# Attention, gated mixing and two dense layers on one core: all pairs of heads run before the dense layers instead of among them

## The chip, the cores and the metric

The kernel runs on one core of a Trainium2 chip. Its time is the device time of one execution in microseconds (us). The version before takes 784.71 us, the median of three runs (782.33 to 784.92). The engines are named as the profile names them: PE (TensorE, matmuls), PEld (its weight loads), DVE (VectorE), ACT (ScalarE), POOL (GpSimd) and SP (the queue that issues most transfers).

## What is computed

Four batches of 448 tokens, 12 heads of 64 channels. Sigmoid attention gives x; a causal convolution of 5 taps makes a gate on x; the gated projection goes through `w_out`; a token mixer and a channel MLP follow, each with a residual.

```python
scores = q @ k.T / sqrt(64) - log(448)           # per batch and head
x = sigmoid(scores) @ v                          # (4, 448, 768) after joining the heads
gate = sigmoid(conv5(x, conv_w))                 # depthwise, causal
x2 = (gate * (x @ w_val)) @ w_out
h  = relu(x2.T @ w_tok1) @ w_tok2                # 448 -> 256 -> 448, over tokens
u  = x2 + h.T
out = u + relu(u @ w_ch1) @ w_ch2                # 768 -> 1536 -> 768, over channels
```

The six weight matrices come as 64-bit words in memory and are decoded on the chip.

## The kernel before

Two heads make a pair; a batch has 6 pairs, all four have 24 (`NPT`). For a pair, `scores` (L235) does, for each of three chunks of 128 keys, two fp32 matmuls that use 64 of PE's 128 rows each, and a sigmoid on ACT (L232); `scores_last` (L244) does the remaining 64 keys of two pairs. `av` (L254) and `av_last` (L264) multiply by v into a PSUM tile `psy`, and `evict` (L272) moves the result to an `xb` tile. An fp32 matmul shows as two records in the trace.

A dense product is done in fp32r with each operand split into a high and a low part: three matmuls for one. `proj` (L354) is the projection by `w_val` (`sel` 0, "val") or `w_out` (`sel` 1); one column block j takes 18 matmuls, issued in three parts. `transp` (L395), `tok1` (L409) and `tok2` (L422) are the token mixer. `dense_steps(b)` (L350) lists these steps for a batch: the six val blocks, then w_out blocks, transposes, tok1 and tok2; the last three tok2 steps are carried into the next batch.

A weight of 128 rows is decoded by `decode_parts` (L103) in four parts: masks (three DVE instructions), rebase (one ACT), low (three DVE), high (one ACT). 18 tiles belong to `w_val`, `w_out`, `w_tok1` and `w_tok2`; the 24 tiles of the channel MLP are decoded later by `dec_ch` (L711). The x of a pair goes through `post_parts` (L315): convolution (`conv`, five DVE instructions), a split (ACT high, DVE low) and the gate's sigmoid.

The order of work is written by hand in a table `PLAN` (L25), by pairs: pairs 0 to 11 in `lead` (L552), two pairs a turn, with decoding between and the convolution of batch 0; pairs 12 to 15 in `lead_val` (L610) with the val blocks of batch 0 and the rest of the decoding; pairs 16 to 18 with the rest of batch 0; 19 to 21 with batch 1; 22 and 23 with batch 2; then val of batch 3. `weave` (L495) deals dense steps out between the pairs, `post` (L502) does the convolutions of later batches. From pair 6 on, x goes to memory (`xscr`, L284, on SP) and comes back (`x_back`, L309).

PSUM in `lead` has three double tiles for scores and two `psy` tiles. From pair 12 on, there are two double tiles for scores (`psa`), two `psy` tiles, and two tiles (`psd`) for dense steps. The steps of batch 3 behind val run in the tail, with six tiles (`psw`, L762); there the decoding of the first three blocks of channel weights (`CHAN_LEFT`) and the first channel products are placed among them. The channel MLP (`ch1` L728, `ch2` L744) follows for 4 batches of 12 blocks.

`lead` and `lead_val` stand under `tc.manual_schedule()`: each engine gets its instructions in the order written. Behind it the scheduler orders them by priority.

```python
    with tc.high_priority(-CHAN_LOW):
        for fc in range(CHAN_LEFT):
            dec_ch(fc, early if fc == 0 else ())
    for n, (_, fn) in enumerate(os):
        if n in CHAN_AT:
            ch1(0, 0, *CHAN_AT[n])
        fn()
```

Of the kernel before, what the change touches and what calls it, by code (L numbers as in the profile page):

```python
# [18 lines left out]
A_BUFS = 3  # L19
Q_BUFS = 3  # L20
# [18 lines left out]
def tile_kernel(ctx, tc, qT, kT, v, w_val, conv_w, w_out, w_tok1, w_tok2, w_ch1, w_ch2, out):  # L39
# [163 lines left out]
    def load_qk(i):  # L203
        b, p = divmod(i, NP)
        h0 = 2 * p
        q = attn.tile([P, S], F32, tag="q", bufs=Q_BUFS, name="q")
        k = attn.tile([P, S], F32, tag="k", bufs=Q_BUFS, name="k")
# [19 lines left out]
    def sigmoid(ps, tag, bufs):  # L227
        if tag == "g":
            a = f(mid.tile([P, 2, S], F32R, tag="g", bufs=6, name="ga"))
        else:  # L230
            a = attn.tile([P, 2, S], F32, tag=tag, bufs=bufs, name=tag)
# [3 lines left out]
    def scores(i, c, lead=False):  # L235
        q, k = qk_t[i]
        ps = pa["pool"].tile([P, 2, 512], F32, tag="s", bufs=pa["s"], name="pss")
# [3 lines left out]
        a_t[i, c] = sigmoid(ps, "g", 6) if lead else sigmoid(ps, "a", A_BUFS)  # L241


    def scores_last(i):  # L244
        ps = pa["pool"].tile([P, 2, 512], F32, tag="s", bufs=pa["s"], name="psl")
# [6 lines left out]
        a_t[i, NF] = sigmoid(ps, "al", 1)  # L252

    def av(i):  # L254
        vn = v_t.pop(i)
        y = pa["pool"].tile([P, 512], F32, tag="y", bufs=2, name="psy")
# [15 lines left out]
    def evict(i, on_vector=False, stays=False):  # L272
        y = y_t.pop(i)[:, :S]
        t = attn.tile([P, PAD + S], F32, tag="xb", bufs=4, name="xb")
# [8 lines left out]
        if not stays:  # L283
            nc.sync.dma_start(xscr[i], x)  # L284
            posts.append(i)

    def step_av(i):
        av(i)
        if i % 2:
            av_last(i - 1)  # L290
            evict(i - 1)
            evict(i)

    def step_loads(i):
        if i + 2 < NPT:
            load_v(i + 2)
        if i % 2 and i + 1 < NPT:
            load_vl(i + 1)

    def step_scores(i):  # L300
        n = i + 1
        if n == NPT:
            return [], []
        todo = [lambda c=c: scores(n, c) for c in range(NF)]
        if i % 2:
            todo = [lambda: scores_last(n)] + todo
        return todo[:2], todo[2:]

    def x_back(i):  # L309
        x = attn.tile([P, PAD + S], F32, tag="xb", bufs=4, name="xb")  # L310
        nc.gpsimd.memset(x[:, :PAD], 0.0)
        nc.sync.dma_start(x[:, PAD:], xscr[i])
        x_t[i] = x

    def post_parts(i):  # L315
# [6 lines left out]
        def conv():  # L322
            nc.vector.tensor_scalar(
                out=acc, in0=x[:, :S], scalar1=cw[:, p * KW : p * KW + 1], scalar2=None, op0=ALU.mult
            )
            for t in range(1, KW):
                nc.vector.scalar_tensor_tensor(  # L327
                    out=acc, in0=x[:, t : t + S], scalar=cw[:, p * KW + t : p * KW + t + 1], in1=acc,
                    op0=ALU.mult, op1=ALU.add,
# [11 lines left out]
        return conv, high, low, last  # L341

    def post_pair(i):
        for part in post_parts(i):
            part()


    carry = []

    def dense_steps(b):  # L350
# [3 lines left out]
        def proj(sel, j, part):  # L354
# [16 lines left out]
            if sel == 0:  # L371
                g = gate_t.pop(b * NP + j)

                gv[j] = t = mid.tile([P, 2, S], F32R, tag="g", bufs=6, name="gv")

                def mul():
                    nc.vector.tensor_tensor(out=g, in0=ps[:, :S], in1=g, op=ALU.mult)  # L377

                def high():
                    nc.scalar.activation(out=t[:, 0], in_=g, func=AF.Copy)  # L380

                def low():
                    nc.vector.tensor_tensor(out=t[:, 1], in0=g, in1=f(t[:, 0]), op=ALU.subtract)

                if dn.get("hold") is None:
                    for fn in (mul, high, low):
                        fn()
                else:
                    dn["hold"].append((mul, high, low))
# [48 lines left out]
        def pj(sel, j):  # L438
            return [(5 if b + sel == 0 else 11, lambda part=part: proj(sel, j, part)) for part in range(3)]

        def tr(j):
            return [(10, lambda: transp(j))]

        def t1(half, t):
            return [(20, lambda: tok1(half, t))]
# [4 lines left out]
        held = [carry.pop(0) for _ in range(len(carry))]  # L450
        steps = []
        for j in range(KD):
            steps += pj(0, j)
            if j in (0, 1, KD - 1) and held:
                steps.append(held.pop(0))
        nval = len(steps)
        steps += pj(1, 0) + pj(1, 1) + tr(0) + pj(1, 2) + tr(1) + pj(1, 3) + tr(2) + pj(1, 4)
        steps += t1(0, 0) + t1(0, 1) + pj(1, 5) + tr(3) + t2(0) + tr(4) + t2(1) + tr(5) + t2(2)
        steps += t1(1, 0) + t1(1, 1)
        if b + 1 < B:  # L460
            carry.extend(t2(3) + t2(4) + t2(5))
        else:
            steps += t2(3) + t2(4) + t2(5)
        return steps, nval
# [4 lines left out]
    decs += [dec_tok1(dec, c) for c in range(NF + 1)] + [dec_tok2(dec, c) for c in range(KT)]  # L469
# [7 lines left out]
    def dec_go():  # L477
        if raws:
            raw, go = raws.pop(0)
            for part in go(raw):  # L480
                part()
            dec_load()

# [6 lines left out]
    pend, posts = [], []  # L490
    total = emitted = 0
    val_done = -1
    back = NP

    def weave(frac):  # L495
        nonlocal emitted
        while pend and (emitted < total * frac or not pend[0][0]):
            n, fn = pend.pop(0)
            emitted += n
            fn()  # L500

    def post(most):  # L502
        nonlocal back
        while posts and most and posts[0] // NP <= val_done + 1:
            i = posts.pop(0)
            while back <= i + 1 and back in posts + [i]:
                x_back(back)
                back += 1
            post_pair(i)
            most -= 1  # L510

    def late():
        while raws:
            dec_go()
        dec.release()
        dn["late"] = tc.alloc_tile_pool(name="late", bufs=1, side="right")

    def mark(b):
        nonlocal val_done
        val_done = b  # L520

    rest_of = {}
    pairs0 = PLAN[0][2]

# [317 lines left out]
```

## Time and profile before

| | |
|---|---|
| runs | 782.33, 784.71, 784.92 us |
| profiled execution, its own time | 784.53 us |
| span of that execution | 782.8 us |
| PE busy | 760.2 us (97%) |
| PEld busy | 604.0 us (77%) |
| DVE busy | 385.1 us (49%) |
| ACT busy | 264.2 us (34%) |
| mean granted TensorE clock | 0.997 |

The profile counts PE as busy from the start of a matmul to its modelled end, and matmuls overlap: 18 records can be 3.65 us or 5.5 us of continuous busy time. How well PE is used is therefore read from how many records lie in a stretch, not from the busy share. Stretches are named below by their start and end in us from the start of the span. The columns of a stretch are: its length, then busy us and number of instructions for PE, PEld, DVE, ACT and POOL, then the granted clock (1.00 is 2.4 GHz, 0.50 is 1.2 GHz), the share of the DMA engines' time, and GB/s.

### The profile page before, as it was taken

To read this page: it belongs to the slowest core of one execution; us is meant where nothing else is said; L and a number is where in the kernel's file an instruction comes from. 1 tells how busy PE (TensorE), PEld (TensorE's weight loads), DVE (VectorE), ACT (ScalarE), POOL (GpSimd) and SP (SyncE) were. 2 spreads that over 40 slices of the span, in tenths; PEclk is the share of its full clock that TensorE was granted. 3 is DMA by queue.
4 is the path that set the end of the run, shared out by engine and by line. 5 is a ranking of instruction groups with operands and counts; after the bars stand their busy time and mean duration, and the time that the engine had idled before them with its cause. 6 is when DMAs were issued, how large, how long until landed. Compare 5 with 4: busy or idle time off the path is not lost.

```text
span 782.8 us, 9546 instructions
## 1 busy us (share of the span) xinstructions
PE 760.2 (97%) x3776; PEld 604.0 (77%) x3776; DVE 385.1 (49%) x671; ACT 264.2 (34%) x397; POOL 26.9 (3%) x67
## 2 busy tenths in 40 slices
PE   7999999999999999999999999999999999999998
PEld 3333556566876688788988998899999999999997
DVE  4987778632631743485696899960003100220002
ACT  6888657433323421332442344430002100200000
POOL 1001110000000000000001000000000000000000
PEclk9999999999999999999999999999999999999999
DMA  8667745112300210213533445460002400050001
GB/s 292 203 191 241 247 129 153 60 49 75 103 23 23 74 36 25 83 58 129 197 123 111 158 166 162 161 212 1 1 0 75 138 1 0 27 174 1 0 1 71
DMA packets 48957, 77.73 MB, mean 99 GB/s; under 512 B 4352, under 2 KB 44304, under 8 KB 48912
## 3 DMA queue, kind: packets, MB, share of 16 engines
q1 hardware_dynamic: 45552, 62.54, 24.7%
q0 software_dynamic: 3360, 14.58, 5.5%
q8 instruction: 30, 0.49, 0.3%
q14 instruction: 15, 0.12, 0.1%
HBM read 61.96 MB, written 15.14 MB: 98 GB/s over the span
## 4 chain that ended last, share of the span: by engine, by line
PE 64%; DVE 15%; issue 13%; DMA 3%; ACT 3%; POOL 1%; SPq 0%; POOLq 0%; DVEq 0%; ACTq 0%
PE psh L734 18%; PE pso L750 18%; PE psd L365 13%; PE psy L261 5%; PE pss L240 4%; DVE gate L327 4%; DVE dec_a L124 2%; PE pst L431 2%; DVE raw L114 2%; PE pst L418 1%; DMA xb<-xscr 1%; DVE wch L128 1%; DVE dec_e L127 1%; DVE dec_a L112 1%; DVE dec_c L113 1%
## 5 line engine op out<-in xcount | busy, mean ns | idle before, releaser
L734 PE MATMUL psh<-us,wch 128*128 128x448 f32 x864 | 184.8, 366 | 0.9 <-ACT wch L136 0.6
L750 PE MATMUL pso<-r,wch 128*128 128x448 f32 x864 | 184.0, 366 | 0.6 <-ACT r L88 0.6
L734 PEld LDWEIGHTS psh<-us,wch 128*128 128x128 f32 x864 | 162.1, 188 | 16.0 <-ACT wch L136 1.6
L750 PEld LDWEIGHTS pso<-r,wch 128*128 128x128 f32 x864 | 162.1, 188 | 14.9 <-ACT r L88 1.0
L90 DVE SCALAR_TENSOR_TENSOR r<-psh,r 128x448 fp32r<-128x448 f32 x48 | 29.9, 624 | 211.0 <-ACT r L88 210.7
L88 ACT ACTIVATE r<-psh 128x448 fp32r<-128x448 f32 x48 | 26.1, 543 | 225.7 <-PE psh L734 225.4
L365 PE MATMUL psd<-gv,w 128*128 128x448 f32 x432 | 95.7, 375 | 4.0 <-ACT x2T L392 2.6
L365 PEld LDWEIGHTS psd<-gv,w 128*128 128x128 f32 x432 | 81.1, 191 | 19.2 <-ACT x2T L392 3.8
L365 PE MATMUL psd<-xs,w 128*128 128x448 f32 x432 | 92.5, 369 | 0.5 <-DVE gate L377 0.5
L365 PEld LDWEIGHTS psd<-xs,w 128*128 128x128 f32 x432 | 80.0, 188 | 15.6 <-issue 5.9
L240 PE MATMUL pss<-q,k 64*128 64x448 f32 x288 | 68.8, 578 | 4.7 <-DMA k<-kT 4.1
L327 DVE SCALAR_TENSOR_TENSOR gate<-xb,cw,gate 128x448 f32<-128x448 f32 x96 | 64.7, 685 | 1.6
L240 PEld LDWEIGHTS pss<-q,k 64*128 64x128 f32 x288 | 25.6, 190 | 40.4 <-issue 17.2
L119 ACT ACTIVATE dec_a<-dec_a,exp_b 128x768 int32<-128x768 int32 (+3 forms) x43 | 37.6, 877 | 48.8 <-DVE dec_a L112 47.2
L124 DVE SCALAR_TENSOR_TENSOR dec_a<-raw,dec_a 128x768 int32<-128x768 int32 (+2 forms) x42 | 37.3, 889 | 14.2 <-ACT dec_a L119 14.2
L232 ACT ACTIVATE a<-pss,bias_s 128x896 f32<-128x896 f32 x36 | 35.0, 1006 | 24.0 <-PE pss L240 21.3
L114 DVE SCALAR_TENSOR_TENSOR raw<-raw,dec_c 128x768 f32<-128x768 uint32 (+2 forms) x42 | 37.6, 895 | 1.2
L261 PE MATMUL psy<-a,v 128*64 128x448 f32 x144 | 34.0, 550 | 1.7 <-ACT a L232 1.7
L232 ACT ACTIVATE ga<-pss,bias_s 128x896 f32<-128x896 f32 x36 | 33.2, 1019 | 4.1 <-PE pss L240 4.1
L377 DVE TENSOR_TENSOR gate<-psd,gate 128x448 f32<-128x448 f32 x24 | 15.0, 623 | 39.6 <-PE psd L365 39.5
L418 PE MATMUL pst<-x,wt1H 128*128 128x384 f32 x112 | 30.2, 339 | 1.7 <-ACT x2T L392 1.0
L136 ACT ACTIVATE wch<-dec_a 128x768 fp32r<-128x768 f32 x24 | 20.3, 846 | 29.6 <-DVE dec_a L124 22.5
(71 smaller groups left out, 607.4 us busy)
## 6 DMA issues: line engine op xcount, KB each, us to landing
raw<-w_ch SPq DMA_DIRECT2D x24, 768.0 KB, 4.4
q<-qT SPq DMA_DIRECT2D x24, 224.0 KB, 3.6
k<-kT SPq DMA_DIRECT2D x24, 224.0 KB, 3.7
uscr<-x2T POOLq DMA_DIRECT2D x24, 224.0 KB, 2.2
u<-uscr SPq DMA_DIRECT2D x24, 224.0 KB, 3.9
ur<-uscr SPq DMA_DIRECT2D x24, 224.0 KB, 3.2
out<-ur SPq DMA_DIRECT2D x24, 224.0 KB, 2.3
v<-v SPq DMA_DIRECT2D x24, 192.0 KB, 2.7
```

What stands on the lines that cost most here:

```text
L90: nc.vector.scalar_tensor_tensor(out=l_out, in0=src, scalar=0.0, in1=f(h_out), op0=ALU.max, op1=ALU.subtract)
L114: nc.vector.scalar_tensor_tensor(out=lo.bitcast(F32), in0=lo.bitcast(U32), scalar=2.0**-32, in1=c, op0=ALU.mult, op1=ALU.add)
L119: nc.scalar.activation(out=t["a"], in_=t["a"], func=AF.Relu, scale=8.0, bias=exp_b)
L124: nc.vector.scalar_tensor_tensor(out=a, in0=hi, scalar=-0x80000000, in1=a, op0=ALU.bitwise_and, op1=ALU.bitwise_or)
L232: nc.scalar.activation(out=a, in_=ps[:, :, :S], func=AF.Sigmoid, bias=bias_s, scale=QK_SCALE)
L240: nc.tensor.matmul(ps[:, j, :S], k[rows, c * P : (c + 1) * P], q[rows], start=True, stop=True)
L261: nc.tensor.matmul(y[cols, :S], vn[:, c, cols], a[:, j], start=c == 0, stop=False)
L327: nc.vector.scalar_tensor_tensor(out=acc, in0=x[:, t : t + S], scalar=cw[:, p * KW + t : p * KW + t + 1], in1=acc, op0=ALU.mult, op1=ALU.add,)
L365: nc.tensor.matmul(ps[:, :S], w(a, kk), s[:, c, :], start=kk == 0 and n == 0, stop=kk == KD - 1 and n == 2,)
L418: nc.tensor.matmul(ps[:, :HALF], a, x[:, m], start=n == 0, stop=n == len(mm) - 1)
L734: nc.tensor.matmul(ps[:, :S], wch[fc][:, 0, a, kk * P : (kk + 1) * P], us_t[b, kk][:, c, :], start=kk == 0 and n == 0, stop=kk == KD - 1 a ...
L750: nc.tensor.matmul(acc[j][:, :S], wch[fc][:, 1, a, j * P : (j + 1) * P], r[:, c, :], start=fc == 0 and n == 0, stop=fc == KF - 1 and n == 2,)
```

## The change

`PLAN`, `lead_val`, `post`, the `hold` list and the carrying of steps are gone. `lead` runs over all 24 pairs, two a turn, in twelve turns, and holds the whole decoding of the 18 tiles (`DEC_LEAD` says how many masks a turn begins); the small tiles of `w_tok1` and `w_tok2` are put between those of `w_out`, so that a turn that begins two has one large and one small tile. All of it, the dense steps of batches 0 to 2 and val of batch 3 included, is now under the manual order.

After the last pair the three double tiles of the scores are given to six tiles `psw` for dense steps. The dense steps of a batch run alone: val, then w_out with the token mixer. The two tok1 steps and three tok2 steps that end a batch are put between the val blocks of the next. Convolutions of batch b + 1 are cut into single instructions and dealt out by weight among the w_out steps of batch b; x comes back from memory four pairs ahead. The tail keeps its text; the channel products take the two `psy` tiles.

```diff
-PLAN = (
-    (None, "", range(0, 12)),
-    (0, "v", range(12, 16)),
-    (0, "o", range(16, 19)),
-    (1, "vo", range(19, 22)),
-    (2, "vo", range(22, 24)),
-    (3, "v", ()),
-)
-DEC_LEAD = (1, 1, 1, 1, 1, 2, 1)
-DEC_VAL = (1, 1, 1, 1, 1, 1, 2, 2)
+DEC_LEAD = (1, 1, 1, 1, 1, 2, 2, 2, 2, 2, 2, 1, 0)
...
+    xbp = tc.alloc_tile_pool(name="xbp", bufs=1, side="left")
-    psl = tc.alloc_tile_pool(name="psl", bufs=2, space=bass.MemoryType.PSUM)
-    pa = {"pool": psl, "s": 3}
+    psy = tc.alloc_tile_pool(name="psy", bufs=2, space=bass.MemoryType.PSUM)
+    pss = tc.alloc_tile_pool(name="pss", bufs=3, space=bass.MemoryType.PSUM)
...
+        val = [pj(0, j) for j in range(KD)]
+        outs = pj(1, 0) + pj(1, 1) + tr(0) + pj(1, 2) + tr(1) + pj(1, 3) + tr(2) + pj(1, 4)
+        outs += t1(0, 0) + t1(0, 1) + pj(1, 5) + tr(3) + t2(0) + tr(4) + t2(1) + tr(5) + t2(2)
+        return val, outs, t1(1, 0) + t1(1, 1), t2(3) + t2(4) + t2(5)
...
-    decs += [dec_tok1(dec, c) for c in range(NF + 1)] + [dec_tok2(dec, c) for c in range(KT)]
+    for n, t in enumerate([dec_tok1(dec, c) for c in range(NF + 1)] + [dec_tok2(dec, c) for c in range(KT)]):
+        decs.insert(6 + 2 * n, t)
...
-        for n, p in enumerate(pairs0[::2]):
+        for n, p in enumerate(range(0, NPT, 2)):
...
             for i in (p, p + 1):
                 evict(i, i > p, p < NP)
             conved = [post_parts(i) for i in (p, p + 1)] if p < NP else []
...
+    def post_ops(b):
+        ops, gates = [], []
+        for i in range(b * NP, (b + 1) * NP):
+            parts = {}
+            def first(i=i, parts=parts):
+                parts["all"] = post_parts(i)
+                parts["all"][0][0]()
+                parts["all"][1]()
+            ops.append(first)
+            for t in range(1, KW):
+                ops.append(lambda t=t, parts=parts: parts["all"][0][t]())
+                if t == 2:
+                    ops += gates
+                    gates = [lambda parts=parts: parts["all"][3]()]
+            def end(i=i, parts=parts):
+                parts["all"][2]()
+                if i + 4 < NPT:
+                    x_back(i + 4)
+            ops.append(end)
+        return ops + gates
+
+    def weave(steps, ops):
+        total = sum(n for n, _ in steps)
+        count, at, done = len(ops), 0, 0
+        for n, fn in steps:
+            fn()
+            at += n
+            while done < count * at // total:
+                ops[done]()
+                done += 1
...
     with tc.manual_schedule():
         lead()
+        pss.release()
+        psw = tc.alloc_tile_pool(name="psw", bufs=6, space=bass.MemoryType.PSUM)
+        pd.update(pool=psw, n=6)
+        attn.release()
+        dec.release()
+        dn["late"] = tc.alloc_tile_pool(name="late", bufs=1, side="right")
+        for i in range(NP, NP + 4):
+            x_back(i)
+        back1, back2 = [], []
+        for b in range(B):
+            val, outs, t1, t2 = dense_steps(b)
+            weave(val[0] + back1 + sum(val[1:], []) + back2, [])
+            if b + 1 < B:
+                weave(outs, post_ops(b + 1))
+            else:
+                os = outs + t1 + t2
+            back1, back2 = t1, t2
+        xbp.release()
...
-            part["ps"] = psd.tile([P, 512], F32, tag="d", bufs=2, name="psh")
+            part["ps"] = psy.tile([P, 512], F32, tag="y", bufs=2, name="psh")
```

## Rows read from the trace of the kernel before

**Rows 1.** Page, busy time by engine: us, share of the span, instructions.
```profile
PE 760.2 (97%) x3776; PEld 604.0 (77%) x3776; DVE 385.1 (49%) x671; ACT 264.2 (34%) x397; POOL 26.9 (3%) x67
```

**Rows 2.** Busy time by stretch: attention, mixed, last dense steps, channels.
```profile
57.24:79.44 22.20, 20.38 (x118) 7.31 (x116) 14.13 (x20) 18.69 (x24) 2.05 (x3) 1.00 0.78 245
79.44:320.95 241.51, 235.99 (x1152) 166.36 (x1152) 122.67 (x237) 95.70 (x149) 13.92 (x36) 0.99 0.25 79
379.68:427.65 47.97, 45.11 (x231) 40.05 (x230) 38.49 (x68) 18.88 (x31) 3.04 (x6) 1.00 0.44 149
427.65:520.00 92.35, 90.81 (x440) 81.81 (x439) 85.45 (x125) 38.22 (x51) 0.96 (x2) 1.00 0.49 162
```

**Rows 3.** Timeline of PE in the lead: start, length, line, tiles, count, [idle before].
```profile
11.34 4.73 PE L261 MATMUL psy<-ga,v 128*64 128x448 f32 x24
...
45.10 4.73 PE L261 MATMUL psy<-ga,v 128*64 128x448 f32 x24
...
57.24 4.73 PE L261 MATMUL psy<-ga,v 128*64 128x448 f32 x24
...
62.70 0.93 PE L251 MATMUL psl<-q,k 64*64 64x448 f32 x8
...
68.50 4.73 PE L261 MATMUL psy<-ga,v 128*64 128x448 f32 x24
```

**Rows 4.** Timeline of ACT in a turn that finishes two large tiles.
```profile
64.69 5.50 ACT L232 ACTIVATE ga<-pss,bias_s 128x896 f32<-128x896 f32 x6
...
74.52 0.84 ACT L136 ACTIVATE w<-dec_a 128x768 fp32r<-128x768 f32 x1 [1.61 <-DVE dec_a L124]
...
76.58 2.81 ACT L232 ACTIVATE a<-pss,bias_s 128x896 f32<-128x896 f32 x3
```

**Rows 5.** Groups by line and shape: the DVE and ACT steps of a small tile.
```profile
L124 DVE SCALAR_TENSOR_TENSOR dec_a<-raw,dec_a 128x256 int32<-128x256 int32 x4 | 1.7, 422 | 0.5 <-ACT dec_a L119 0.5
L136 ACT ACTIVATE wt1H<-dec_a 128x256 fp32r<-128x256 f32 x4 | 1.6, 409 | 1.3 <-DVE dec_a L124 1.3
```

**Rows 6.** Transfers: queue, count, size, median us from issue to landing; and SP's timeline.
```profile
k<-kT SPq DMA_DIRECT2D x24, 224.0 KB, 3.7
raw<-w_tok POOLq DMA_DIRECT2D x3, 256.0 KB, 3.1
...
67.20 0.56 SPq L208 DMA_DIRECT2D q<-qT  x1
```

**Rows 7.** Timeline of PE: dense steps beside attention, and dense steps by themselves.
```profile
83.55 2.71 PE L365 MATMUL psd<-xs,w 128*128 128x448 f32 x12
86.19 1.02 PE L240 MATMUL pss<-q,k 64*128 64x448 f32 x4
...
160.19 5.51 PE L365 MATMUL psd<-gv,w 128*128 128x448 f32 x18 [1.47 <-ACT x2T L392]
...
363.87 14.75 PE L365 MATMUL psd<-xs,w 128*128 128x448 f32 x72
378.45 0.56 PE L431 MATMUL pst<-wt2H,h 128*128 128x448 f32 x2
...
379.68 7.60 PE L365 MATMUL psd<-gv,w 128*128 128x448 f32 x36
387.12 0.60 PE L401 MATMUL pst<-ident,x2T 128*128 128x128 f32 x4
387.48 0.85 PE L365 MATMUL psd<-gv,w 128*128 128x448 f32 x3
```

**Rows 8.** Chain that ended last, in order of time: a tok1 pair and a tok2 step.
```profile
275.60 3.82 PE pst L418 x22
...
291.50 1.23 PE pst L431 x6
```

**Rows 9.** Timeline of DVE: decoding channel weights around the end of val, batch 3.
```profile
353.94 0.56 DVE L112 TENSOR_SCALAR dec_a<-raw 128x768 int32<-128x768 int32 x1 [1.13 <-DMA raw<-w_ch]
...
379.45 0.95 DVE L128 SCALAR_TENSOR_TENSOR wch<-raw,dec_e 128x768 fp32r<-128x768 f32 x1
```

More of the change, by code (lines that the diff above doesn't have):

```diff
@@ L225, in load_vl, with sigmoid, scores @@
         vl_t[i] = t
[L227 to L231, printed above, removed]
+    def sigmoid(ps, a):
         nc.scalar.activation(out=a, in_=ps[:, :, :S], func=AF.Sigmoid, bias=bias_s, scale=QK_SCALE)
         return a
-    def scores(i, c, lead=False):
+    def scores(i, c):
         q, k = qk_t[i]
-        ps = pa["pool"].tile([P, 2, 512], F32, tag="s", bufs=pa["s"], name="pss")
+        ps = pss.tile([P, 2, 512], F32, tag="s", bufs=3, name="pss")
         for j in range(2):
@@ L240, in scores @@
             nc.tensor.matmul(ps[:, j, :S], k[rows, c * P : (c + 1) * P], q[rows], start=True, stop=True)
-        a_t[i, c] = sigmoid(ps, "g", 6) if lead else sigmoid(ps, "a", A_BUFS)
+        a = mid.tile([P, 2, S], F32R, tag="g", bufs=6, name="ga")
+        a_t[i, c] = sigmoid(ps, f(a))
     def scores_last(i):
-        ps = pa["pool"].tile([P, 2, 512], F32, tag="s", bufs=pa["s"], name="psl")
+        ps = pss.tile([P, 2, 512], F32, tag="s", bufs=3, name="psl")
         for h in range(2):
@@ L284, in evict @@
             nc.sync.dma_start(xscr[i], x)
[L285 to L307, printed above, removed]
     def x_back(i):
-        x = attn.tile([P, PAD + S], F32, tag="xb", bufs=4, name="xb")
+        x = xbp.tile([P, PAD + S], F32, tag="xb", bufs=4, name="xb")
         nc.gpsimd.memset(x[:, :PAD], 0.0)
@@ L339, in last @@
             nc.scalar.activation(out=acc, in_=acc, func=AF.Sigmoid)
[L341 to L348, printed above, removed]
+        return [lambda t=t: conv(t) for t in range(KW)], high, low, last
     def dense_steps(b):
@@ L372, in proj @@
                 g = gate_t.pop(b * NP + j)
[L374 to L389, printed above, removed]
+                nc.vector.tensor_tensor(out=g, in0=ps[:, :S], in1=g, op=ALU.mult)
+                gv[j] = mid.tile([P, 2, S], F32R, tag="g", bufs=6, name="gv")
+                split(gv[j][:, 0], gv[j][:, 1], g)
             else:
@@ L489, in tile_kernel @@
     make_identity(nc, ident)
[L490 to L523, printed above, removed]
-    begun, going = [], []
+    begun = []
     def dec_masks(n):
@@ L559, in lead @@
         for c in range(NF):
-            scores(0, c, True)
+            scores(0, c)
         for part in cgo(craw):
@@ L565, in lead @@
         for c in range(NF):
-            scores(1, c, True)
+            scores(1, c)
         load_qk(4)
@@ L577, in lead @@
                 parts[1]()
-            for parts, _ in done:
+            for parts in done:
                 parts[2]()
@@ L584, in lead @@
                 fn()
-            for parts, _ in done:
+            for parts in done:
                 parts[3]()
@@ new lines, in lead @@
+            if more:
+                scores_last(p + 2)
+                for i in (p + 2, p + 3):
+                    for c in range(NF):
+                        scores(i, c)
+                    if i + 3 < NPT:
+                        load_qk(i + 3)
+            for parts in conved:
+                for fn in parts[0]:
+                    fn()
+        assert not (conved or gates or begun or raws or decs)
+    def post_ops(b):
[18 more added lines that the diff above has]
+        return ops + gates
@@ L693, in tile_kernel @@
-    psa.release()
-    attn.release()
+        pss.release()
[12 more added lines that the diff above has]
+                weave(outs, post_ops(b + 1))
+            else:
+                os = outs + t1 + t2
+            back1, back2 = t1, t2
@@ L808, in tile_kernel @@
     pso.release()
-    psd.release()
+    psy.release()
 def kernel(q, k, v, moe_w_val, moe_conv_w, moe_w_out, moe2_w_tok1, moe2_w_tok2, moe2_w_ch1, moe2_w_ch2):
```

166 lines of the change are left out of this document (21 added, 145 removed).

## The prediction

> **What bounds the kernel now.** I read the busy times first [rows 1]: PE is busy 97% of the span, so nothing but PE's own time can give much. But PEld is at 77%, and a busy PE is not a full one, so the second view is the table by stretch [rows 2], read by records per us. In the channel part, from 427.65 to 520, 440 records lie in 92.35 us, 0.210 us each, and each of them is a full dense matmul. In the mixed stretch, 79.44 to 320.95, where attention and dense steps share PE, 1152 lie in 241.51 us, 0.2097 us each, but many of these are the half-size records of attention, transposes and tok1, which cost less elsewhere. The reader should see that this stretch looks full by busy time (235.99 us) and is not.
>
> The third view is PE's timeline, which gives the price of each piece when it is undisturbed. In the lead, three turns of two pairs start 33.76 us apart in all, 11.25 us each, and a later one takes 68.50 - 57.24 = 11.26 us [rows 3]. Dense: 72 val matmuls run from 363.87 to 378.45, 14.58 us, so a val block of 18 is 3.65 us; 36 matmuls by `w_out` run from 379.68 to 387.12, 7.44 us, so a block is 3.72 us; four transposes take 387.48 - 387.12 = 0.36 us [rows 7]; two tok1 steps are 3.82 us, a tok2 step 1.23 us [rows 8]. Beside attention the same 12 val matmuls take 86.19 - 83.55 = 2.64 us instead of 12 x 0.2025 = 2.43, and one block of `w_out` takes over 5 us behind a wait of 1.47 us for ACT [rows 7]. With these prices I can build the stretch of the new order from pieces that the trace has already run.
>
> **The change part by part.** *Attention and decoding, all in the lead.* The first product with v starts at 11.34; nothing ahead of it changes. There are twelve turns; eleven end in scores for the next pairs, and the last has none. A full turn is 11.26 us [rows 3]. One turn of the six before is longer, 57.24 - 45.10 = 12.14 us, 0.88 more; it follows the three turns with convolutions, which stay, so I keep this once. The last turn is av and av_last, 62.70 - 57.24 = 5.46 us [rows 3]. Sum: 11.34 + 11 x 11.26 + 0.88 + 5.46 = 141.5 us.
>
> Whether 11.26 holds for turns 6 to 10, which finish two decoded tiles each, is the first open cost. In a turn of before that finishes two large tiles ACT is the longer chain: its six sigmoids start at 64.69, those of the next pairs at 76.58, 11.89 us, and ahead of the second tile's last step it waits 1.61 us for DVE [rows 4]. In the new order the second tile is small (256 or 448 wide), and its steps on that chain are 0.422 us on DVE and 0.409 us on ACT [rows 5]. The large one's ACT step is 0.84 [rows 4], twice that, and I take the same ratio for its DVE step, so some 0.43 + 0.43 us come off: 11.0 us, under PE's 11.26. PE stays the bound, by 0.2 to 0.3 us.
>
> Behind this stands a second chain. With three `raw` buffers and two tiles a turn, the second tile's load goes out only when the first tile's low part is done, and DVE waits for it ahead of the copy of `psy`; SP's writes of x wait for this copy, and the loads of q and k stand behind them. In the turn of before that begins at 57.24, q goes out at 67.20 and takes 0.56 us to issue, and the k behind it takes 3.7 us to land [rows 3, 6]: 71.5. The next scores that want it come 11.26 + 5.46 us behind 57.24, at 74.0. So there are 2.5 us of room. That turn began two large masks without waiting; one large mask and a wait for a small load, 3.1 us [rows 6], end by my count about 1 us later. The bounds are 0 and, for six turns that each lose 1.5 us, 9 us; I take 1 us, since the rows leave room. Writing x of pairs 12 to 23 and loading tiles for longer stays far from the DMA limit: the lead's stretch shows a DMA share of 0.78 with large tiles only [rows 2].
>
> PE has no gap between the last av and val of batch 0: the scores' PSUM tiles were read before that av could start, the x of batch 0 was convolved in the first turns, and `w_val` is decoded first. I cost this at nothing; a visible wait for the release of the pools would be under 1 us.
>
> *Batches 0 to 2 alone.* Of one batch: 6 x 3.65 (val) + 6 x 3.72 (w_out) + 6 x 0.36 (transposes) + 2 x 3.82 (tok1) + 6 x 1.23 (tok2) = 61.4 us; three are 184.2. To this come waits at transposes and tok steps, which before had attention work to cover them. The nearest row is the last stretch of dense steps [rows 2], which already runs with six PSUM tiles and no attention: 47.97 us, against 43.2 by the prices (the same without val, plus one channel block of 3.65), so 4.8 us are lost. Bounds: 0 to 4.8 per batch, 0 to 14.4 in all. I take 1.5 per batch, 4.5 in all: in that last stretch ACT and DVE also decode channel weights (DVE busy 38.49 of 47.97) in an order that no one wrote, while in batches 0 to 2 they have one convolution instruction at a time between the dense steps. Those convolutions cost PE nothing as long as DVE keeps up, which in the mixed stretch was busy 122.67 us of 241.51 with decoding besides [rows 2]. The wait that they bring to DVE is for x out of memory, with the copies of the dense steps queued behind it and PE behind these. SP issues that load four pairs ahead, two thirds of a batch's w_out steps, and POOL's memset ahead of it stands only behind writes of tok2 results of earlier steps; I cost this wait at nothing. Without that lead it would be one landing, near the 3.7 us of k [rows 6], per pair.
>
> *Val of batch 3 and the tail.* Val is 6 x 3.65 = 21.9 us. The tail keeps its text, so I take its measured 47.97 us, and from 427.65 to the end of the span, 782.76 - 427.65 = 355.1 us. One thing moves: before, DVE started channel weights at 353.94, during val of batch 3, and only the write of the first tile waited to 379.45 [rows 9]. Now val of batch 3 stands in the manual order, and the decoding comes behind it on DVE. Six tiles at 85.45 us / 18 = 4.7 us [rows 2] are 28 us; some 4 to 5 us of that move into the last dense stretch, which has 47.97 - 38.49 = 9.5 us of DVE idle. I cost it at nothing, with bounds of -2 (loads come earlier) and +5.
>
> Sum: 141.5 + 1 + 184.2 + 4.5 + 21.9 + 47.97 + 355.1 = 756.2 us of span; the profiled run took 1.73 us beyond its span (784.53 and 782.8), which gives 757.9, so 758 us. The profiled run lies within 0.2 us of the median, so no further shift.
>
> The drain of PE fits this: 12 matmuls beside attention lose 0.21 us [rows 7]. The Trainium skill (TensorEngine Tiling (Array Packing), "Key Properties") says that changing the tiling mode drains the engine, and attention's half arrays are such a mode. By the rule the change saves one drain wherever attention and dense steps alternated; the sum above holds these savings already, through the undisturbed prices.
>
> **The rivals.** *Stalls of dense steps alone.* If batches 0 to 2 lose what the last stretch lost, 4.8 us each, 9.9 us are added: 768. For it: transposes follow their projection by one block only, with nothing else to run. Against it: the waits there are behind decoding.
>
> *The lead starves.* If q and k come late in turns 5 to 10, at 1.5 to 2 us each, 9 to 12 us are added: 768 to 770.
>
> *Decoding becomes the bound, no change.* If the scheduler places the six first tiles of channel weights behind all of batch 3's dense steps, PE waits for 28 us of decoding, less the 3.65 us of a channel block: 758 + 25 = 783. For it: the decoding has lower priority and its early start is gone. Against it: DVE's idle time in that stretch and the same text of the tail.
>
> *The clock falls, slower.* Attention alone fills half of the array per matmul. If the granted clock fell to 1.2 GHz in the 62 us of attention that the change adds to the lead (79 to 141 us), every us of work there would cost another: up to 820 us. It decides from 27 us at half clock on, the whole gain. Against it: the lead's rows show 1.00 with attention only, and the mixed stretch, the one with gaps, shows 0.99 [rows 2]. The Trainium skill (TensorE: Matmul & The Clock Gate, "What's actually happening") has it that the throttled clock is the default and activity releases it; the trace agrees, 1.00 where PE runs without gaps.
>
> **How the numbers follow.** Forecast, 750 to 764: 0.60. Stalls, about 768: 0.15. Lead starves, about 769: 0.10. Both or more, 774 to 782: 0.03. Decoding, about 783: 0.05. Clock, 790 and above: 0.07. The likeliest is 758. The range goes from 750 (no waits, and the tail 2 to 3 us better) to 774 (either of the first two rivals with decoding 5 us late); it leaves out the last three and a little below. A measurement of this kernel tells about 0.3% from no change, 2.4 us: faster 0.88, same 0.05, slower 0.07.
>
> **What would show it.** PE's last av near 141 us; turns 11.3 us apart to the end, and ACT's sigmoids starting 0.2 us behind the scores; val of batch 0 right behind; the batches 62 to 63 us apart; the last tok2 near 400 us; the channel part 355 us as before. Wrong would be: turns of 12.5 us with PE waiting for q, k or ACT; dense steps with waits of over a us at each transpose; channel matmuls that wait for DVE behind 400 us; a granted clock of 0.50 before 141 us.

## The result, and the profile after

The changed kernel takes 756.89 us (median of four runs, 754.59 to 758.20) against 784.25 us for the kernel before on the same chip (four runs): a ratio of 0.9652, with a 95% interval from 0.9621 to 0.9682. Its profiled execution took 756.25 us, with a span of 754.5 us; before, the span was 782.8 us. The gain of 28.3 us of span is the difference that the text below accounts for.

The busy times by engine from the page of the changed kernel answer to [rows 1]. PE's busy time fell by 19.2 us although it runs the same 3776 matmuls, DVE's rose by 8.5 us, and the others' changed by less than 4:

```profile
PE 741.0 (98%) x3776; PEld 604.3 (80%) x3776; DVE 393.6 (52%) x677; ACT 260.3 (35%) x391; POOL 27.5 (4%) x67
```

The same table by stretch as [rows 2], for the stretches of the changed kernel: attention from the first product with v, the dense steps of batches 0 to 2 with val of batch 3, the last dense steps, and the first part of the channel products.

```profile
12.87:143.60 130.73, 130.56 (x739) 47.97 (x737) 92.07 (x159) 108.26 (x138) 10.51 (x18) 1.00 0.69 215
143.60:353.74 210.14, 207.79 (x1073) 192.15 (x1069) 136.40 (x254) 63.66 (x120) 10.33 (x31) 1.00 0.18 57
353.74:399.25 45.51, 44.28 (x232) 40.28 (x230) 37.14 (x66) 16.92 (x27) 4.17 (x8) 1.00 0.45 154
399.25:491.00 91.75, 89.71 (x436) 81.25 (x435) 85.12 (x124) 38.45 (x51) 0.96 (x2) 1.00 0.49 161
```

The reader sees two uniform stages where there was one mixed stretch. The last dense step ends at 399.25 instead of 427.65, 28.4 us sooner; from there to the end it is 355.25 us, before 355.1. So the whole gain lies ahead of the end of the dense steps.

PE's timeline shows the hand-over from attention to dense work and the clean prices of the dense steps, as [rows 7] did for before:

```profile
138.03 4.73 PE L248 MATMUL psy<-ga,v 128*64 128x448 f32 x24
142.69 0.98 PE L257 MATMUL psy<-al,vl 64*64 64x448 f32 x8
143.60 2.70 PE L321 MATMUL psd<-xs,w 128*128 128x448 f32 x12
...
165.59 7.59 PE L321 MATMUL psd<-gv,w 128*128 128x448 f32 x36
173.02 0.60 PE L344 MATMUL pst<-ident,x2T 128*128 128x128 f32 x4
173.37 0.45 PE L321 MATMUL psd<-gv,w 128*128 128x448 f32 x1
```

Val of batch 0 starts 0.91 us after the last group of attention did, with no wait. The 108 val matmuls take 21.99 us, and four transposes 0.35 us. One wait comes back in each of batches 1 to 3, in the first val block, which takes 4.70 us instead of 3.65; 0.78 us of the 1.05 show as a wait:

```profile
197.85 3.61 PE L321 MATMUL psd<-xs,w 128*128 128x448 f32 x17
202.24 0.47 PE L321 MATMUL psd<-xs,w 128*128 128x448 f32 x1 [0.78 <-DVE xs L299]
202.55 0.34 PE L361 MATMUL pst<-x,wt1H 128*128 128x384 f32 x1
```

From the records of PE I also counted where before lost its time. Each group of matmuls is priced at the undisturbed rate of its kind, and what it took beyond that is lost. In the mixed stretch (79.44 to 320.95) this is 24.6 us. In it, PE goes 62 times from attention to dense work or back. Groups ending in such a change that lost under 0.6 us each sum to 11.5 us; six single losses of 0.85 to 2.1 us sum to 9.1; the rest is 4.0. From 320.95 to 427.65 another 9.9 us are lost, none of them at a change. After, the dense steps from 143.6 to 399.25 lose 6.2 us in all. These sums hang on the prices, the one for the scores above all.

One loss in the mixed stretch is neither a change nor a wait. Two matmuls that each use half of the array run together when they stand side by side, their records starting within 0.01 us of each other. One alone takes as long as the two: in the trace of before, the four records of two `scores` matmuls and the two records of a single one both take 0.95 us up to the next matmul.

```profile
86.19 1.02 PE L240 MATMUL pss<-q,k 64*128 64x448 f32 x4
87.14 2.70 PE L365 MATMUL psd<-xs,w 128*128 128x448 f32 x12
...
179.78 1.02 PE L240 MATMUL pss<-q,k 64*128 64x448 f32 x2
180.73 0.68 PE L431 MATMUL pst<-wt2H,h 128*128 128x448 f32 x2
```

In the mixed stretch 14 matmuls of attention run alone like this, in the lead of either kernel none. At some 0.38 us each (half of what two cost in the run lump below) that is about 5 of the 24.6 us, an estimate; some 2.5 of them stand within the 11.5 above.

### The profile page after: what moved, and what is told of

The parts are those of the page before. It is cut to its first block, busy times and chain, and to the rows that moved or that the text cites. A ratio compares the mean times of both kernels' runs of the same rounds, so it can differ in the third digit from the quotient of the medians.

```text
span 754.5 us, 9599 instructions
## 1 busy us (share of the span) xinstructions
PE 741.0 (98%) x3776; PEld 604.3 (80%) x3776; DVE 393.6 (52%) x677; ACT 260.3 (35%) x391; POOL 27.5 (4%) x67
## 4 chain that ended last, share of the span: by engine, by line
PE 67%; DVE 14%; issue 13%; DMA 3%; ACT 1%; POOL 1%; SPq 0%; POOLq 0%; DVEq 0%; ACTq 0%
PE psh L582 19%; PE pso L598 18%; PE psd L321 15%; PE pss L226 6%; PE psy L248 5%; DVE gate L291 3%; PE pst L361 2%; DMA raw<-w_ch 2%; DVE raw L102 2%; DVE dec_a L112 2%; DVE wch L116 1%; PE psl L238 1%; DVE dec_a L100 1%; PE pst L374 1%; PE psy L257 1%
## 5 line engine op out<-in xcount | busy, mean ns | idle before, releaser
L321 PE MATMUL psd<-gv,w 128*128 128x448 f32 x432 | 92.8, 369 | 0.0
L321 PE MATMUL psd<-xs,w 128*128 128x448 f32 x432 | 89.6, 366 | 2.3 <-DVE xs L299 2.3
L217 ACT ACTIVATE ga<-pss,bias_s 128x896 f32<-128x896 f32 x72 | 66.4, 1019 | 4.7 <-PE pss L226 4.7
L226 PE MATMUL pss<-q,k 64*128 64x448 f32 x288 | 63.0, 579 | 4.3 <-DMA k<-kT 4.1
L248 PE MATMUL psy<-ga,v 128*64 128x448 f32 x288 | 56.8, 543 | 0.0
L248 PEld LDWEIGHTS psy<-ga,v 128*64 128x64 f32 x288 | 19.6, 137 | 35.7 <-issue 29.9
L76 ACT ACTIVATE gv<-gate 128x448 fp32r<-128x448 f32 x24 | 13.8, 577 | 61.7 <-DVE gate L330 61.7
```

What stands on the lines that cost most here:

```text
L76: nc.scalar.activation(out=h_out, in_=src, func=AF.Relu if relu else AF.Copy)
L226: nc.tensor.matmul(ps[:, j, :S], k[rows, c * P : (c + 1) * P], q[rows], start=True, stop=True)
L248: nc.tensor.matmul(y[cols, :S], vn[:, c, cols], a[:, j], start=c == 0, stop=False)
L321: nc.tensor.matmul(ps[:, :S], w(a, kk), s[:, c, :], start=kk == 0 and n == 0, stop=kk == KD - 1 and n == 2,)
```

## The experiments

All times are medians of four runs. The kernel before, run beside them, had medians from 782.94 to 785.11 us.

| label | what is changed | us | ratio to before (95%) |
|---|---|---|---|
| (the change) | | 756.89 | 0.9652 (0.9621 to 0.9682) |
| lump | 36 added matmuls in one group | 770.96 | 0.9839 (0.9818 to 0.9860) |
| spread | the same, dealt out | 777.32 | 0.9918 (0.9897 to 0.9939) |
| psum2 | two PSUM tiles for dense steps | 769.06 | 0.9818 (0.9797 to 0.9838) |
| psum3 | three | 757.99 | 0.9673 (0.9659 to 0.9688) |
| spread2 | spread and psum2 together | 790.22 | 1.0071 (1.0052 to 1.0090) |
| bigpairs | small tiles decoded last | 759.50 | 0.9690 (0.9667 to 0.9714) |
| whole | convolutions in one piece | 778.15 | 0.9919 (0.9898 to 0.9940) |
| beforehand | before, ordered by hand | 831.32 | 1.0599 (1.0565 to 1.0632) |
| autodense | dense steps ordered by the scheduler | 752.82 | 0.9604 (0.9579 to 0.9628) |
| sooner | convolutions end sooner | 752.84 | 0.9602 (0.9588 to 0.9616) |
| low0 | sooner, channel decoding not lower | 753.33 | 0.9604 (0.9583 to 0.9626) |

The theory was that before lost time on PE itself, at each change between attention and dense work, and through waits that mixed work brings. The rivals were that the gain is the number of PSUM tiles, or the order by hand.

### What a change between attention and dense work costs: lump and spread

```diff
+    def extra(n):
+        m = xs_t[0]
+        for _ in range(n):
+            for j in range(2):
+                rows = slice(j * D, (j + 1) * D)
+                nc.tensor.matmul(spare[j][:, :S], ident[rows], f(m[rows, 0, :]), start=True, stop=True)
...
+            if b == 0:
+                extra(18)                                     # lump
...
+                val = [[(n, lambda fn=fn: (extra(1), fn())) for n, fn in v] for v in val]   # spread
```

> The changed kernel with 36 added fp32 matmuls of 64 rows (72 records) on PE in one group ahead of val of batch 0; their results are not used. No engine waits for them and they wait for none. Both theories: 72 x 0.206 = 14.8 us more, 771 to 773 us.

> The same 36 added matmuls, two ahead of each of the 18 parts of val of batch 0, so that PE changes between half-array and full-array matmuls 36 times. Theory (each alternation costs PE itself some 0.185 us; 62 of them in the mixed stretch of before would be 11.5 of its 24.6 lost us): 6 to 7 us over the kernel with one group, 777 to 780 us. Rival (alternation is free; all that was lost were waits for buffers and other engines): the same as one group within 1 us.

Measured: 770.96 and 777.32 us, 6.4 us apart; the spans of the profiled executions, 769.1 and 775.8, are 6.7 apart. Lump costs 14.1 us, just under what was expected. In both kernels the first added matmul does wait once, 0.72 us, for a copy out of `psy`. PE's timeline in lump:

```profile
143.52 13.85 PE L529 MATMUL spare<-xs,ident 64*128 64x448 f32 x72 [0.72 <-ACT xb L269]
157.30 22.15 PE L321 MATMUL psd<-xs,w 128*128 128x448 f32 x108
179.29 3.04 PE L321 MATMUL psd<-gv,w 128*128 128x448 f32 x14
```

and in spread:

```profile
147.14 1.48 PE L321 MATMUL psd<-xs,w 128*128 128x448 f32 x6
148.55 1.02 PE L529 MATMUL spare<-xs,ident 64*128 64x448 f32 x4
149.51 0.47 PE L321 MATMUL psd<-xs,w 128*128 128x448 f32 x1
```

In one group, a half-array record takes 13.78 / 72 = 0.191 us and a dense one 21.99 / 108 = 0.2036. Alternating, four and six take 149.51 - 147.14 = 2.37 us instead of 4 x 0.191 + 6 x 0.2036 = 1.99. That is 0.38 us for two changes, 0.19 us each, with no wait on any engine shown. The rival is out: alternation is not free. Dealt out, PE changes 35 times instead of once, 34 times more and not 36 as expected, so 6.4 to 6.7 us are 0.19 to 0.20 us a change. 62 changes at that price are 11.6 to 12.2 us, and the mixed stretch of before lost 11.5 at its changes, or some 9, by the same prices, without the matmuls that ran alone. The added matmuls have the form of the scores (64*128); changes to and from the products with v (128*64) were not tried by themselves.

### The PSUM tiles: psum2, psum3, spread2

```diff
-        psw = tc.alloc_tile_pool(name="psw", bufs=6, space=bass.MemoryType.PSUM)
-        pd.update(pool=psw, n=6)
+        psw = tc.alloc_tile_pool(name="psw", bufs=2, space=bass.MemoryType.PSUM)
+        pd.update(pool=psw, n=2)
...
         xbp.release()
+        psw.release()
+        psw = tc.alloc_tile_pool(name="psw", bufs=6, space=bass.MemoryType.PSUM)
+        pd.update(pool=psw, n=6)
```

> The changed kernel with two PSUM tiles instead of six for the dense steps up to val of batch 3; everything else stays. Theory (most of the gain is the order: no alternation of attention and dense steps on PE, and waits that the order hides): some waits come back at the transposes and tok steps of batches 0 to 2, as in the stretch from 320.95 to 379.68 of before, 1 to 3 us a batch, 3 to 9 us in all, 760 to 766 us. Rival (the gain is mostly the third and following PSUM tiles): 15 us or more come back, 772 to 785 us.

Measured: 769.06 us, 12.2 more than with six tiles, between what the two expected. PE's timeline of this kernel shows where:

```profile
173.39 0.60 PE L344 MATMUL pst<-ident,x2T 128*128 128x128 f32 x4
174.19 1.08 PE L321 MATMUL psd<-gv,w 128*128 128x448 f32 x4 [0.20 <-ACT x2T L335]
...
197.41 0.63 PE L344 MATMUL pst<-ident,x2T 128*128 128x128 f32 x4 [0.49 <-DVE x L348]
198.69 0.67 PE L374 MATMUL pst<-wt2H,h 128*128 128x448 f32 x2 [0.65 <-DVE x2T L378]
```

Four transposes keep PE for 0.80 us until the next block, not 0.36, because that block's tile is still being copied by ACT; in the chain of transposes and tok2 steps each waits for the copy of the step before the last. A batch takes 66.2 us instead of 62.7.

> The changed kernel with three PSUM tiles instead of six for the dense steps up to val of batch 3. Two tiles gave 769.1 us, 12.2 more than six, 3.5 us a batch at the transposes (0.80 us for four instead of 0.36) and the tok2 steps. Theory (with two tiles a step waits for the copy of the step before the last; one more tile covers a copy of 0.6 us): nearly all of it goes with the third tile, 757 to 760 us. Rival (each further tile gives its share): 765 to 767 us.

Measured: 757.99 us. The third tile takes back nearly all, 11.1 of 12.2 us; the rival, a share for each tile, is out.

> The kernel with the 36 added matmuls dealt out among val of batch 0 (777.3 us) and, besides, two PSUM tiles instead of six for the dense steps up to val of batch 3 (769.1 us alone, 12.2 over the changed kernel's 756.9). Theory (alternation and tiles are separate costs): they add, 777.3 + 12.2 = 789.5, 788 to 791 us; then 62 alternations at 0.187 us and two tiles, 11.6 + 12.2, account for 24 of the 27 to 28 us between the two kernels. Rival (one hides the other, as PE's extra time at each change covers the wait for a tile): 783 to 786 us.

Measured: 790.22 us, 12.9 over spread. The two costs add. That this is no faster than the kernel before says little, since 14.1 us of it are the added matmuls themselves (lump). Together 11.6 and 12.2 us are 23.8 of the 27.4 us between the kernels. This sum is a reconstruction and not shown: the 12.2 us are the price of two tiles in the new order, and no run has more than two with attention among the dense steps. The count on the traces divides the gain otherwise: 24.6 + 9.9 - 6.2 = 28.3 us, as much as the spans differ by, of which some 9 lie at changes, about 5 in matmuls that ran alone, and the rest in waits and small losses.

### The decoding in the lead: bigpairs

```diff
-    for n, t in enumerate([dec_tok1(dec, c) for c in range(NF + 1)] + [dec_tok2(dec, c) for c in range(KT)]):
-        decs.insert(6 + 2 * n, t)
+    decs += [dec_tok1(dec, c) for c in range(NF + 1)] + [dec_tok2(dec, c) for c in range(KT)]
```

> The changed kernel with the small tiles of w_tok1 and w_tok2 decoded last, as before the change, so that some turns of the lead finish two large tiles. The prediction's step: such a turn is bound by ACT and DVE, 11.9 us instead of 11.26, and the second large tile's load (5 us) comes late for its masks, so three or four turns of 11.9 to 13.5 us, 2 to 7 us more in all, 759 to 764 us. Rival (PE alone sets the turn, whatever is decoded): no change.

Measured: 759.50 us, 2.6 more. The runs go from 757.45 to 761.85 and the interval of the ratio overlaps that of the change, so this is not clear of noise. The profiled execution is the slowest of the four. Its table by stretch, one turn a row:

```profile
58.55:69.81 11.26, 11.26 (x66) 4.18 (x65) 6.82 (x10) 9.57 (x13) 0.77 (x1) 1.00 0.79 252
69.81:81.69 11.88, 11.74 (x66) 4.04 (x64) 7.41 (x11) 10.05 (x13) 1.29 (x2) 1.00 0.74 252
81.69:93.59 11.90, 11.90 (x66) 4.27 (x64) 8.71 (x12) 10.06 (x13) 1.30 (x2) 1.00 0.80 255
93.59:108.76 15.17, 13.13 (x67) 4.68 (x65) 10.68 (x17) 10.36 (x13) 1.32 (x2) 0.89 0.68 214
108.76:120.02 11.26, 11.26 (x66) 4.19 (x64) 5.12 (x12) 9.34 (x13) 1.58 (x3) 1.00 0.65 187
```

Two turns take 11.88 and 11.90 us, as the chain of ACT in [rows 4] gave (11.89); their sigmoids start 89.78 - 77.88 = 11.90 us apart. The third takes 15.17. There the second chain has run out of room. DVE waits 4.23 us for a tile, and the copy of `psy` stands behind its masks. PE's next product with v starts 0.10 us after that copy ends; the profile names no releaser for it (`issue`), so that it waited for the copy is read from the order. The granted clock then falls in the same turn, after PE had waited for 2.04 us. The rows of the timeline, of ACT, DVE and PE:

```profile
77.88 5.50 ACT L217 ACTIVATE ga<-pss,bias_s 128x896 f32<-128x896 f32 x6
89.78 5.50 ACT L217 ACTIVATE ga<-pss,bias_s 128x896 f32<-128x896 f32 x6
...
95.44 0.57 DVE L100 TENSOR_SCALAR dec_a<-raw 128x768 int32<-128x768 int32 x1 [4.23 <-DMA raw<-w_out]
97.39 0.62 DVE L267 COPY xb<-psy 128x448 f32<-128x448 f32 x1
...
98.11 4.05 PE L248 MATMUL psy<-ga,v 128*64 128x448 f32 x12 [2.04 <-issue]
```

So PE is not alone in setting the turn: two turns lose 1.3 us together, as the prediction's step worked out. The third turn's 3.9 us are one execution's; it is the only one of the four with a mean clock under 1.00 (0.998).

### Who orders, and in what pieces: beforehand, autodense, sooner, whole

Beforehand puts the mixed stretch of the kernel before under the manual order:

```diff
-    for b, parts, pairs in PLAN[2:]:
+    with tc.manual_schedule():
+        for b, parts, pairs in PLAN[2:]:
...
```

> The kernel before with the mixed stretch from pair 16 to val of batch 3 under the manual order too, in the order in which its text issues it; nothing else is changed. Theory (alternation and waits of mixed work make the difference, not who orders): 780 to 792 us, the 62 alternations still there. Rival (the scheduler's order of the mixed stretch was what the change removed): 770 us or less.

Measured: 831.32 us, which neither expected; it lies 39 us above the theory's upper end. The text's order of mixed work is far worse than the scheduler's. Part of it is the clock: the mean granted clock of the execution is 0.964, against 0.997, so some 60 of 831 us ran at 1.2 GHz (2 x 0.036 x 831). That would cost 30 us if PE had worked all through them; by the records it sat idle for some 17 of them, which leaves about 20 us, an estimate. PE's idle time grew by more, from 22.6 us of the span (782.8 - 760.2) to 59.1 (831.0 - 771.9). Two stretches of 40 us from the table show it beside PE's lower busy time:

```profile
120.00:160.00 40.00, 33.58 (x150) 23.86 (x152) 31.42 (x62) 17.71 (x31) 1.15 (x5) 0.87 0.24 70
160.00:200.00 40.00, 31.67 (x152) 22.13 (x144) 10.34 (x21) 14.27 (x22) 1.19 (x3) 0.87 0.22 69
```

One cause is in ACT's timeline:

```profile
143.39 0.58 ACT L339 ACTIVATE gate<-gate 128x448 f32<-128x448 f32 x1 [2.74 <-DVE gate L327]
143.88 0.96 ACT L392 ACTIVATE x2T<-psd 128x448 f32<-128x448 f32 x2
```

and it is the largest row of the list of PE's waits (us in total, times, longest):

```profile
PE psd L365 <- ACT x2T L392: 17.4, 5, 7.7
```

ACT waits 2.74 us for a convolution on DVE ahead of the gate's sigmoid; the copies of two dense results stand behind it, and PE waits for those. In the text a pair's convolution and its sigmoid are one piece.

Whole puts the convolutions of the changed kernel back into such pieces, and changes nothing else:

```diff
-                if t == 2:
-                    ops += gates
-                    gates = [lambda parts=parts: parts["all"][3]()]
...
             ops.append(end)
-        return ops + gates
+            ops.append(lambda parts=parts: parts["all"][3]())
+            group = ops[-6 - 1 :]
+            ops[-6 - 1 :] = [lambda group=group: [fn() for fn in group]]
+        return ops
```

> The changed kernel with the convolution of a pair put among the w_out steps in one piece (five DVE instructions, low part, and the gate's sigmoid on ACT right behind) instead of in single instructions with the sigmoid held back; the same work, six pieces a batch. In the kernel before with its mixed stretch ordered by hand (831.3 us), ACT waits up to 2.7 us for such a group and the copies of the dense steps stand behind it. Theory (cutting the convolution is what makes an order by hand cheap here): PE waits 0.5 to 2 us at several steps of each batch, 8 to 25 us in all, 765 to 782 us. Rival (with no attention among them the dense steps have slack enough for whole pieces): 757 to 760 us.

Measured: 778.15 us, 21.3 more: most of the gain is lost. ACT's timeline:

```profile
179.99 0.58 ACT L302 ACTIVATE gate<-gate 128x448 f32<-128x448 f32 x1 [3.10 <-DVE gate L291]
180.47 0.58 ACT L346 ACTIVATE x<-pst 128x512 fp32r<-128x512 f32 x1
180.95 0.54 ACT L335 ACTIVATE x2T<-psd 128x448 f32<-128x448 f32 x1
```

The first two rows of the list of PE's waits:

```profile
PE psd L321 <- DVE xs L299: 10.6, 3, 3.5
PE psd L321 <- ACT x L346: 4.5, 3, 1.5
```

The six tiles cover ACT's 3.10 us there (PE shows no wait near 180), but the last piece of a batch ends far behind the w_out steps, and PE waits up to 3.5 us in the first val block; the mean clock is 0.988. Set beside the changed kernel record by record, PE loses nothing through the first three pieces of a batch. Behind the fourth and the fifth, among the last transposes and tok2 steps, it loses 0.9 and 1.7 us more, at the sixth 2.7, and the clock of 1.2 GHz that follows costs 1.4 to 2.4: 6.8 to 7.8 us a batch. So it is shown that whole pieces at the end of a batch cost 21.3 us, more than the alternation or the tiles alone. Whether whole pieces would cost this too if they ended sooner, as in the kernel sooner below, was not tried, so that the cutting by itself is a condition of the new order is not shown.

Autodense takes the dense steps out of the manual order, by moving their code out of the block:

```diff
     with tc.manual_schedule():
         lead()
-        pss.release()
...
+    pss.release()
...
```

> The changed kernel with only the attention lead in the order written by hand; the dense steps of batches 0 to 2 and val of batch 3 are ordered by the scheduler, as nearly all of them were before. Theory (alternation and waits of the mixed stretch): the order by hand is worth little, 755 to 762 us. Rival (the gain is the order by hand): 770 us or more.

Sooner keeps the order by hand and lets the convolutions end earlier:

```diff
-            while done < count * at // total:
+            while done < min(count, count * at * 10 // (9 * total)):
```

> The changed kernel with the convolution instructions dealt out over the first nine tenths of the w_out steps instead of all of them. In the trace of the changed kernel PE waits 1.05 us in the first val block of batches 1 to 3 (4.70 us instead of 3.65) for the low part of x of the last pair. Theory (that wait is the place of the last convolution instructions in DVE's order): it goes in all three batches, 3 us less, 753 to 754 us. Rival (DVE is behind with work by then, and the place does not matter): no change, 756 to 758 us.

Measured: 752.82 and 752.84 us, both about 4 us faster than the change itself, and the fastest kernels here; autodense came out 2 us below the range of its theory. The first val block of batch 1 in sooner:

```profile
196.65 3.81 PE L321 MATMUL psd<-xs,w 128*128 128x448 f32 x18
200.30 0.34 PE L361 MATMUL pst<-x,wt1H 128*128 128x384 f32 x1
```

It takes 3.65 us, and the same holds in batches 2 and 3: the wait of 1.05 us was the place of the last convolution instructions in DVE's order, and nothing else. These three blocks are 3.1 of the 4 us. In autodense the scheduler moves them, with the same effect. The order of the dense steps by hand is thus not what the change gained by: without it the kernel is faster still.

### What is left in the tail: low0

```diff
-CHAN_LOW = 600
+CHAN_LOW = 0
```

> The changed kernel with the convolution instructions dealt out sooner (752.8 us) and, besides, the decoding of the channel weights at normal priority in the tail instead of 600 lower. PE still loses some 2.5 us in the last dense steps and 4 to 5 us around 460 to 480 of the span, where DVE decodes without a pause. Theory (in that stretch DVE's 18 tiles behind the last dense step set the end; priority does not start them sooner, since their place in memory comes free only then): 752 to 756 us, no gain. Rival (decoding is late because it stands behind other work on DVE): 747 to 750 us.

Measured: 753.33 us, no gain over sooner. In the stretch of the table where PE still loses some 2 us, DVE is busy nearly all the time in both. In sooner:

```profile
455.00:480.00 25.00, 22.84 (x110) 19.99 (x109) 23.14 (x34) 10.85 (x16) 0.00 (x0) 1.00 0.39 128
```

and in low0:

```profile
455.00:480.00 25.00, 22.97 (x107) 19.33 (x106) 22.70 (x34) 11.39 (x16) 0.00 (x0) 1.00 0.39 133
```

This fits decoding as the limit there. That the memory for the tiles comes free too late was not tried.

## Why the prediction was right, step by step

| step | predicted us | measured us |
|---|---|---|
| first product with v | 11.34 | 12.87 |
| eleven turns | 123.86 + 0.88 + 1 | 125.16 |
| last turn | 5.46 | 5.57 |
| batches 0 to 2 and val of batch 3 | 184.2 + 4.5 + 21.9 = 210.6 | 210.14 |
| last dense steps | 47.97 | 45.51 |
| channel products to the end | 355.1 | 355.25 |
| span | 756.2 | 754.5 |

**The method held.** The new order is made of pieces that before had already run undisturbed, and nine of its eleven turns and its blocks take what [rows 3, 7, 8] said, to 0.1 us. The forecast, 758, is 1.1 us off the median. That it came so close is in part luck: the start was 1.5 us longer and the tail 2.5 us shorter than forecast, and the sum held neither. One figure of its reading is off in the last place (241.51 / 1152 is 0.2096), which changes nothing.

**The start** was 1.5 us later, and not for its loads: the first scores begin at 4.09 us instead of 4.13. PE's first twelve records take 4.78 us up to what follows them instead of 3.83, while the later twelve take 2.46 in both. Before, and then the changed kernel:

```profile
4.13 3.90 PE L240 MATMUL pss<-q,k 64*128 64x448 f32 x12 [4.13 <-DMA k<-kT]
8.88 2.53 PE L240 MATMUL pss<-q,k 64*128 64x448 f32 x12
...
4.09 4.85 PE L226 MATMUL pss<-q,k 64*128 64x448 f32 x12 [4.09 <-DMA k<-kT]
10.41 2.53 PE L226 MATMUL pss<-q,k 64*128 64x448 f32 x12
```

At first two records start some 0.72 us after the two before them, later 0.37. The trace's records of a granted clock begin, with 1.00, at 6.94 us in before, 7.49 in spread, 9.10 in lump and 10.20 in the changed kernel; the first product with v comes at 11.34, 11.59, 12.27 and 12.87. So the start goes with the time at which PE reaches full speed, which varies from one execution to the next, spread's and lump's starts having the same text.

**The turns.** One turn after the convolutions took 11.92 us (0.66 for the 0.88 expected) and one later took 11.85, 0.59 for the 1 us set aside. The later one lost it at `scores_last`, where spread's trace, in the same turn, has PE wait 0.19 us for k: the place that the second chain gave. That the turn stays at 11.26 was right for the reason given: bigpairs takes the small tiles away and gets the 11.9 us that the step had worked out for two large ones, and then the second chain (load, masks, copy of `psy`) that the step had feared. That step had looked for the harm at q and k; in bigpairs it came at the copy, and PE's wait was, by the order, for a free `psy` tile.

**The stalls of dense steps** were the right size, 4.0 us for 4.5, for a largely wrong reason, which is luck. I put 1.5 us a batch at the transposes and tok steps; they show no wait. A loss of 1.05 us stands in the first val block of each later batch, at the low part of the last convolved pair. The prediction had left the end of a batch's convolutions out. The reason why the rival "stalls of dense steps alone" fell is the one given: in the last stretch of before the waits, 2.8 us, were for copies on DVE and ACT, which decode there, and batches 0 to 2 have no decoding; autodense, whose batches the scheduler orders too, has no such waits in them either. But two conditions were taken as given that carry much of the gain: six tiles (psum2, 12.2 us) and convolutions in single instructions that end in time (whole, 21.3 us). A change with the same idea and without the one would have brought half of the gain, without the other less than a quarter.

**The tail** took 2.5 us less than its copy from before, a little beyond my bound of -2; its DVE did not come under the pressure that I had bounded at +5. I had the decoding of channel weights come behind val of batch 3 on DVE. It began during val, which runs from 323.27 to 353.74:

```profile
332.51 0.56 DVE L100 TENSOR_SCALAR dec_a<-raw 128x768 int32<-128x768 int32 x1 [1.29 <-DMA raw<-w_ch]
...
351.02 0.95 DVE L116 SCALAR_TENSOR_TENSOR wch<-raw,dec_e 128x768 fp32r<-128x768 f32 x1
```

So the first tile was written 2.7 us ahead of the last dense steps, in before 0.2 us ahead of them [rows 9], and PE's waits in that stretch fell from 2.8 to 1.2 us. The rival "decoding becomes the bound" did not happen.

**The clock** stayed at 1.00 from the first product with v through all of attention and dense work, so the rival on the other side fell as the rows of the lead said; the row of before that shows 1.00 there was not without gaps, as the prediction has it, since PE is busy for 20.38 of its 22.20 us. It is no idle rival, though: beforehand and whole show a falling clock, and there it comes in or behind waits of PE, while 130 us of half-array matmuls kept 1.00.

**The drain.** The rule of the Trainium skill (TensorEngine Tiling (Array Packing), "Key Properties"), by which a change of the tiling mode drains PE, agrees with spread: 0.19 to 0.20 us at each change with no other wait. That the engine drains in this time no run shows by itself.

## What to carry to other kernels

Price each group of matmuls at its undisturbed rate and look for the loss by stretch; a busy share of 98% hid most of 24.6 us here. Work of two tiling modes on PE belongs in two stages, if each stage alone can be fed: enough PSUM tiles (three did here), and vector work cut or placed so that no copy of a PSUM tile stands behind a whole chain. Keep two half-array matmuls side by side; one alone takes the time of both. Check the end of each hand-made interleaving: the last piece has the least time.

## What the runs showed of the hardware

A change between half-array fp32 matmuls (64*128) and full-array fp32r matmuls costs 0.19 to 0.20 us, and the profile shows no wait for it; it appears only as a longer spacing of records, some 0.1 us more on either side of the change in spread.

A single half-array matmul takes as long as two side by side, 0.95 us up to the next matmul in before.

The granted clock fell behind a wait of PE of 2.04 us in one turn of bigpairs, whose mean is 0.89, and the kernel ordered by hand runs about 60 us at 1.2 GHz. Of its 47 us over the kernel before, about 20 are the clock, an estimate; most of the others are waits.
